# Attention and Fourier mixing on one Trainium2 core: the mixing's even column sums ahead of its odd ones, and cosine products ahead of sine products

## The chip, the cores and the metric

The kernel runs on one core of one Trainium2 chip. The metric is the time of the device for one execution, in microseconds (us). TensorE (PE in the profile, PEld for its weight loads), VectorE (DVE), ScalarE (ACT), GpSimd (POOL) and the DMA queue of SyncE (SP) work beside each other; each runs its own list of instructions in order and waits on semaphores for the others.

## What is computed

Eight batches of eight heads with 576 tokens: attention in which, per row, only scores within tau of the row's maximum are kept. The 512 columns that result per token go through a two-dimensional Fourier transform of which the real part is added, a normalization, and two matrices with a ReLU between them.

```python
scores = scale * np.matmul(q, k.transpose(0, 1, 3, 2))
thresh = np.max(scores, axis=-1, keepdims=True) - tau
scores = np.where(scores >= thresh, scores, -1000000000.0)
attn = np.exp(scores - np.max(scores, axis=-1, keepdims=True))
attn = attn / (np.sum(attn, axis=-1, keepdims=True) + 1e-09)
x = np.matmul(attn, v)                 # then (B,H,S,D) -> (B,S,H*D)
u = x + np.real(np.fft.fft(np.fft.fft(x, axis=1), axis=2))
un = (u - mean(u)) / np.sqrt(var(u) + 1e-06)
out = u + np.maximum(un @ w_ch1, 0.0) @ w_ch2
```

All data is fp32.

## The kernel before

**Order by hand.** The order on every engine is the order in which the program calls its functions; no scheduler moves anything. Generators are advanced at chosen places, so that stages of different batches interleave.

**Attention.** A pair of heads has five steps, t=0 to 4, and a batch has four pairs, so 20 steps (`per_batch`). A step i does, in the loop of the later batches: `scores(i)` (L440; L446 for t=4, which holds the leftover rows of both heads and so is half as large); `softmax_first`, the negated row maxima on VectorE (L520) and behind them the exponentials on ScalarE (L526, with the threshold at L530); `fill(True)`, a share of the matrix work of an earlier batch; `softmax_second`, the masking on VectorE (L540) and the inverse of the sum (L385, L388); the transposes of the weights of step i-1 on TensorE (L587, L605) and their copies on ScalarE (L593, L607), in two parts with a `fill()` between; `softmax_third`, the scaling (L549); at t=3 `prep_pair`, which transposes q and k of the next pair on VectorE (L408 to L411); and a last `fill`. The values are L636, their copy L643 or L645. The scores of step i+1 need the PSUM banks that the masking of step i has read.

**Mixing.** A batch's transform over 576 tokens uses symmetries. `fold_rows` adds and subtracts mirrored halves of the rows of a pair (`half`, L687) and folds them again into `f` (L692 to L703), which has four chunks p and, in each, even columns (the first FW = 304) and odd columns (the next 304). The last pair of a batch is folded on VectorE, the others on GpSimd. `mixing(b)` is a generator for the rest:

- `fold_chunks` adds and subtracts chunks 0 and 2 on VectorE (L718, L719), all 608 columns at once. Chunks 1 and 3 were done on GpSimd before.
- Five additions and folds on VectorE, of 304 columns each, put the sums into place (L744, L740 three times, L749).
- Six products `py` on TensorE (L759): three groups of rows u, for each an even one with the cosine table (three matmuls) and an odd one with the sine table (two). ScalarE copies each from PSUM (L764; for an even one also a single column, L769).
- Products over the sequence (`pa`, L776 and L780), additions on VectorE (L796, L797), and the sum with x into `u_t` (L801, L805).

Each `yield` in it is a place where other work comes between. In the later batches `start_batch` puts the mixing of the batch before into the list at t=2 of the first pair; `mix(1)` advances it by one piece behind the masking, a `fill()` by one more. The three pieces of sums go to t=2 behind the masking, to the next `fill()`, and to t=3 ahead of the masking. The first `py` follows at t=3 behind the masking.

```python
        if i % per_batch == 3:
            mix(1)
```

stands for that between `softmax_first` and `fill(True)`. For batch 0 (`second_batch`, `first == 0`) sums and products are called by hand behind the eight matmuls of `column_means` (L360); for the last batch (the tail) three `mix(1)` go between shares of the matrix work, and the rest follows when `ended` is set.

**Matrices.** Both channel products run on TensorE as two-level products with seven multiplications for eight (`ph`, L1203; `po`, L1390). Their sums are spread over the other engines: differences of halves of the hidden rows on GpSimd (L1161), sums and differences of their quarters on VectorE and GpSimd (L1184), gathering on GpSimd (L1255, L1336), partial results out of PSUM on ScalarE (L1402) or VectorE (L1410), and rows with their factor (L883, L888).

**PSUM.** `py`, `pe`, `pw`, `pv`, `pa`, `po`, `ph` share four banks (tag mm); a new tile takes a bank whose last reader has to be done. Scores have four banks of their own.

## Time and profile before

| | |
|---|---|
| median of 3 runs | 1574.97 us (1571.53 to 1575.13) |
| the profiled execution | 1571.58 us, of which the span of instructions is 1569.8 |
| mean granted TensorE clock | 0.996 |
| busy: PE, PEld | 1526.0 us, 1187.1 us |
| busy: DVE, ACT, POOL | 1061.6, 916.4, 777.5 us |
| L759 `py`: matmuls | 240, of 275 ns (median) |
| L718, L719 on DVE, 608 columns | 8 each, 0.78 and 0.79 us (median) |
| L744, L749, 304 columns | 8 each, 0.47 us (median) |
| L740, 304 columns | 24, 0.53 us (median) |

The span runs from the first to the last instruction. A line of the timeline gives the start, the duration, the engine with the line of the code, the operation, the tile written and the tiles read with their sizes, the count, and in brackets the idle time of the engine just ahead of it with what ended it. A line with a count merges equal neighbours: its duration is that of them all. A duration of VectorE can contain time in which it stood.

### The profile page before, as it was taken

Reading aid. Unit: us, or ns where it says so; the run is one execution under the profiler, and the core shown is the slowest. Engines: PE = TensorE matmul, PEld = TensorE weight load, DVE = VectorE, ACT = ScalarE, POOL = GpSimd, SP = SyncE. Lnnn points to the kernel's source line nnn. Section 1 sums busy time; section 2 is a strip of 40 time slices with the busy share of each in tenths; the row PEclk is TensorE's granted clock in tenths of the full one; section 3 lists DMA queues with packets and bytes.
Section 4 is the critical chain, followed back from the end, with each engine's and each line's share of the span. In section 5 each row is a group of like instructions: output and inputs, shape, how many; then the busy total and the mean of one; then the engine's idle time right before and its main releaser. Section 6 shows DMA issues by size and latency. Waiting matters only on the chain.

```text
span 1569.8 us, 27001 instructions
## 1 busy us (share of the span) xinstructions
PE 1526.0 (97%) x9786; PEld 1187.1 (76%) x9786; DVE 1061.6 (68%) x2119; ACT 916.4 (58%) x1921; POOL 777.5 (50%) x962
## 2 busy tenths in 40 slices
PE   8988989999999999999999999999999999999999
PEld 4555545556788778877787778877787878889999
DVE  7987776846869566776577566866577666745546
ACT  6875666554666666656766566657666666232231
POOL 3774553034455652546254724555264625546735
PEclk9999999999999999999999999999999999999999
DMA  6423231646956264634454345635464434646655
GB/s 166 130 58 117 77 90 24 204 147 180 323 154 214 73 188 122 185 111 144 144 173 149 116 135 153 184 103 158 130 185 137 141 118 149 222 141 235 235 201 182
DMA packets 248907, 239.31 MB, mean 152 GB/s; under 512 B 197027, under 2 KB 218533, under 8 KB 228678
## 3 DMA queue, kind: packets, MB, share of 16 engines
q1 hardware_dynamic: 246262, 237.28, 49.6%
q8 instruction: 78, 1.28, 0.3%
q10 hardware_dynamic: 2512, 0.30, 0.1%
q14 instruction: 55, 0.45, 0.1%
HBM read 205.93 MB, written 31.46 MB: 151 GB/s over the span
## 4 chain that ended last, share of the span: by engine, by line
PE 83%; DVE 9%; ACT 4%; issue 1%; DMA 1%; POOL 1%; SPq 0%; ACTq 0%; DVEq 0%
PE ph L1203 24%; PE po L1390 18%; PE pv L636 9%; PE sc L440 9%; PE pw L605 7%; PE po L926 4%; PE ph L902 3%; PE sc L446 2%; PE py L759 2%; PE pa L776 1%; PE pe L587 1%; DVE neg L461 1%; PE pn L851 1%; PE pa L780 1%; PE pd L111 1%
## 5 line engine op out<-in xcount | busy, mean ns | idle before, releaser
L520 DVE TENSOR_REDUCE neg<-sc 128x1 f32<-128x576 f32 x216 | 154.3, 751 | 131.4 <-PE sc L440 118.6
L526 ACT ACTIVATE e<-sc,neg 128x576 f32<-128x576 f32 x216 | 158.5, 734 | 120.7 <-DVE neg L520 120.7
L1390 PE MATMUL po<-w,w_all 128*128 128x128 f32 x1728 | 219.0, 277 | 0.3 <-ACT ends L593 0.3
L1140 DVE TENSOR_TENSOR hs<-ph,hs 128x512 f32<-128x512 f32 (+1 forms) x128 | 105.4, 823 | 161.1 <-PE ph L1203 104.0
L1390 PEld LDWEIGHTS po<-w,w_all 128*128 128x128 f32 x1728 | 204.9, 192 | 9.2 <-issue 6.2
L1149 POOL TENSOR_TENSOR w<-hs 128x512 f32<-128x512 f32 x32 | 42.1, 1320 | 317.8 <-ACT hs L1145 243.9
L540 DVE SCALAR_TENSOR_TENSOR e<-sc,thr,e 128x576 f32<-128x576 f32 x216 | 168.4, 813 | 19.9 <-ACT thr L530 19.6
L1203 PE MATMUL ph<-u_t,w 128*128 128x256 f32 x768 | 180.5, 382 | 0.6 <-DMA w<-f 0.4
L607 ACT COPY e_t<-pw 128x512 f32<-128x512 f32 x256 | 148.7, 595 | 45.8 <-PE pw L605 44.7
L605 PE MATMUL pw<-ident,e 128*128 128x128 f32 x1152 | 169.9, 275 | 5.6 <-ACT ends L593 2.2
L440 PE MATMUL sc<-kT,qT 64*128 64x288 f32 x1024 | 168.1, 431 | 6.6 <-DVE e L477 4.4
L549 ACT ACTIVATE e<-e,den 128x576 f32<-128x576 f32 x216 | 157.5, 775 | 8.5 <-DVE den L388 7.7
L1203 PEld LDWEIGHTS ph<-u_t,w 128*128 128x128 f32 x768 | 141.4, 190 | 23.2 <-issue 4.4
L1203 PE MATMUL ph<-w_all,w 128*128 128x256 f32 x672 | 157.1, 383 | 1.1 <-DVE w_all L1125 1.0
L605 PEld LDWEIGHTS pw<-ident,e 128*128 128x128 f32 x1152 | 135.4, 141 | 21.9 <-issue 5.6
L1203 PEld LDWEIGHTS ph<-w_all,w 128*128 128x128 f32 x672 | 123.6, 190 | 23.7 <-issue 4.9
L1145 ACT ACTIVATE hs<-hs 128x512 f32<-128x512 f32 (+1 forms) x96 | 74.1, 771 | 113.5 <-DVE hs L1140 112.8
L440 PEld LDWEIGHTS sc<-kT,qT 64*128 64x128 f32 x1024 | 95.7, 187 | 57.9 <-issue 26.8
L1255 POOL TENSOR_TENSOR w_all<-w_all 128x128 f32<-128x128 f32 (+2 forms) x160 | 116.9, 747 | 30.3 <-DVE w_all L1410 22.4
L1390 PE MATMUL po<-w,hs 128*128 128x128 f32 x912 | 119.4, 278 | 0.3 <-ACT ends L593 0.3
L1390 PEld LDWEIGHTS po<-w,hs 128*128 128x128 f32 x912 | 109.7, 192 | 9.7 <-issue 7.1
L801 POOL TENSOR_TENSOR u_t<-x,tmp 128x289 f32<-128x289 f32 (+1 forms) x45 | 33.9, 753 | 123.7 <-DVE tmp L796 123.7
(224 smaller groups left out, 2946.7 us busy)
## 6 DMA issues: line engine op xcount, KB each, us to landing
w<-f SPq DMA_DIRECT2D x150, 1024.0 KB, 4.9
hs<-in_moe_w_ch_dram SPq DMA_DIRECT2D x23, 512.0 KB, 5.2
q_in<-in_q_dram SPq DMA_DIRECT2D x128, 72.0 KB, 4.1
out_dram<-u SPq DMA_DIRECT2D x36, 256.0 KB, 2.3
k_in<-in_k_dram SPq DMA_DIRECT2D x124, 72.0 KB, 2.6
v_in<-in_v_dram SPq DMA_DIRECT2D x64, 128.0 KB, 5.0
f<-w SPq DMA_DIRECT2D x14, 512.0 KB, 3.9
f<-w SPq DMA_DIRECT2D x7, 1024.0 KB, 4.8
```

The costliest lines, as they stand in the source:

```text
L440: nc.tensor.matmul(sc[j][:, c, 0:HALF], qT[hp, 128 * t : 128 * t + 128], kT[hp, k0 + HALF * c : k0 + HALF * (c + 1)], start=True, stop=True,)
L520: nc.vector.tensor_reduce(out=neg[:, j : j + 1], in_=sc[j][:, :, 0:HALF], axis=AXIS_XY, op=ALU.max, negate=True,)
L526: nc.scalar.activation(out=ej, in_=sc[j][:, :, 0:HALF], func=ACT.Exp, bias=neg[:, j : j + 1], scale=1.0)
L540: nc.vector.scalar_tensor_tensor(out=ej, in0=sc[j][:, :, 0:HALF], scalar=thr[:, j : j + 1], in1=ej, op0=ALU.is_ge, op1=ALU.mult, accum_out ...
L549: nc.scalar.activation(out=e[:, S * j : S * (j + 1)], in_=e[:, S * j : S * (j + 1)], func=ACT.Copy, scale=den[:, j : j + 1],)
L605: nc.tensor.transpose(pw[:, c, :], e[:, c0 : c0 + 128], ident[:, :])
L607: nc.scalar.copy(e_t[:, 4 * j : 4 * j + 4, qs], pw[:, :, :])
L636: nc.tensor.matmul(pv[64 * j : 64 * j + 64, 0:m], vt[:, 2 * c + j, :], e_t[:, 4 * j + c, 0:m] if c < 4 else ends[:, 0, 0:m], start=(c == 0 ...
L1140: nc.vector.tensor_tensor(out=to, in0=bank, in1=to if other is None else other, op=ALU.add)
L1203: nc.tensor.matmul(bank[:, 256 * q : 256 * q + 256].rearrange("p (two n) -> p two n", two=2), left[:, 256 * c + 128 * q : 256 * c + 128 * ...
L1255: return lambda: eng.tensor_tensor(out=to, in0=to, in1=other, op=ALU.add)
L1390: nc.tensor.matmul(to, lefts[m][j][:, s], right_[:, 128 * s : 128 * (s + 1)], start=jn in (0, 4) and s == 0, stop=s == 3, skip_group_check ...
```

## The change

- `fold_chunks` gets the columns as an argument. `mixing` first sums the even columns only (two instructions of 304 columns), then does the three even folds in one piece, with the third of them moved up; the sums and folds of the odd columns (two and two instructions) stand in the third piece, and there is no `yield` between them and the first product.
- The six products come in the order cosine u=0, 1, 2, then sine u=0, 1, 2.
- The `mix(1)` at t=3 ahead of the masking goes. The third piece, with the first product, is therefore advanced by the `mix(1)` behind the masking, where the first product was.
- For batch 0 the fold of the last pair is split: the even half, the mixing's even sums, then the odd half.
- For the last batch two instead of three `mix(1)` stand between the shares of matrix work.

All else in `fold_rows` is a regrouping that issues the same instructions in the same order. The number of instructions grows by two on VectorE for each batch.

```diff
@@ fold_rows
+        if last and not late:
+            once(0)
+            twice(0)
+            middle()
+            yield
+            once(1)
+            twice(1)
+            return
@@
-    def fold_chunks(eng, b, c):
-        eng.tensor_tensor(out=sums[b][:, c, :], in0=f[:, c, :], in1=f[:, c + 2, :], op=ALU.add)
-        eng.tensor_tensor(
-            out=f[:, c + 2, :], in0=f[:, c, :], in1=f[:, c + 2, :], op=ALU.subtract
-        )
+    def fold_chunks(eng, b, c, cols=slice(0, 2 * FW)):
+        low, high = f[:, c, cols], f[:, c + 2, cols]
+        eng.tensor_tensor(out=sums[b][:, c, cols], in0=low, in1=high, op=ALU.add)
+        eng.tensor_tensor(out=high, in0=low, in1=high, op=ALU.subtract)
@@ mixing
-        fold_chunks(nc.vector, b, 0)
+        fold_chunks(nc.vector, b, 0, E)
         yield 0
...
         fold(f[:, 1, E], s01[:, 1, E], flip, s01[:, 0, E])
+        fold(f[:, 2, E], f[:, 3, E], minus, f[:, 2, E])
         yield 0
-        fold(f[:, 2, E], f[:, 3, E], minus, f[:, 2, E])
+        fold_chunks(nc.vector, b, 0, O)
         fold(f[:, 3, O], f[:, 2, O], plus, f[:, 3, O])
         nc.vector.tensor_tensor(out=f[:, 0, O], in0=s01[:, 0, O], in1=s01[:, 1, O], op=ALU.subtract)
-        yield 0
+        sums.pop(b)
...
-        for u, r, n in ((0, 0, 128), (1, 128, 48), (2, 176, 128)):
-            for odd in range(2):
+        for odd in range(2):
+            for u, r, n in ((0, 0, 128), (1, 128, 48), (2, 176, 128)):
@@ second_batch, first == 0
-            folds.append(fold_rows(n - 1))
-            while folds:
-                fold_more()
+            outer = fold_rows(n - 1)
+            next(outer)
+            start_batch(0)
+            mix(2)
+            next(outer, None)
             load_v(n + 1)
-            start_batch(0)
-            mix(3)
             mix(3)
@@ the loop of the later batches, behind softmax_first
-        if i % per_batch == 3:
-            mix(1)
@@ the tail
-        if n < 3:
+        if n < 2:
             mix(1)
```

More of the change, by code (lines that the diff above doesn't have):

```diff
@@ L685, in fold_rows, with once, twice, middle @@
         eng = nc.vector if last else nc.gpsimd
-        for c, op in enumerate((ALU.add, ALU.subtract)):
-            eng.tensor_tensor(out=half[:, c, 1:HALF], in0=up, in1=down, op=op)
-        yield
-        for c, c0, op in (
-            (0, 0, ALU.add), (0, 161, ALU.subtract), (1, FW, ALU.subtract), (1, FW + 161, ALU.add)
-        ):
-            eng.tensor_tensor(
-                out=f[:, p, c0 : c0 + mid - 1], in0=half[:, c, 1:mid],
-                in1=_reversed(half[:, c, mid + 1 : HALF]), op=op,
-            )
-            if late and last and c0 > 0 and c0 != FW:
-                yield
-        eng.tensor_tensor(
-            out=f[:, p, mid - 1 : mid + 1], in0=_stepped(x, mid, -mid, 2),
-            in1=_stepped(x, 3 * mid, -mid, 2), op=ALU.add,
-        )
-        eng.tensor_tensor(
-            out=_stepped(f[:, p, :], 160, FW, 2), in0=_stepped(x, 0, mid, 2),
-            in1=_stepped(x, HALF, mid, 2), op=ALU.subtract,
-        )
+        def once(c):
+            eng.tensor_tensor(
+                out=half[:, c, 1:HALF], in0=up, in1=down, op=(ALU.add, ALU.subtract)[c]
+            )
+        def twice(c):
+            for c0, op in zip((FW * c, FW * c + 161), (ALU.add, ALU.subtract)[:: 1 - 2 * c]):
+                eng.tensor_tensor(
+                    out=f[:, p, c0 : c0 + mid - 1], in0=half[:, c, 1:mid],
+                    in1=_reversed(half[:, c, mid + 1 : HALF]), op=op,
+                )
+        def middle():
+            eng.tensor_tensor(
+                out=f[:, p, mid - 1 : mid + 1], in0=_stepped(x, mid, -mid, 2),
+                in1=_stepped(x, 3 * mid, -mid, 2), op=ALU.add,
+            )
+            eng.tensor_tensor(
+                out=_stepped(f[:, p, :], 160, FW, 2), in0=_stepped(x, 0, mid, 2),
+                in1=_stepped(x, HALF, mid, 2), op=ALU.subtract,
+            )
+        if last and not late:
[6 more added lines that the diff above has]
+            return
+        once(0)
+        once(1)
+        yield
+        twice(0)
+        if late and last:
+            yield
+        twice(1)
+        if late and last:
+            yield
+        middle()
         yield
@@ L715, in fold_halves @@
         fold_chunks(nc.gpsimd, b, 1)
-    def fold_chunks(eng, b, c):
-        eng.tensor_tensor(out=sums[b][:, c, :], in0=f[:, c, :], in1=f[:, c + 2, :], op=ALU.add)
-        eng.tensor_tensor(
-            out=f[:, c + 2, :], in0=f[:, c, :], in1=f[:, c + 2, :], op=ALU.subtract
-        )
+    def fold_chunks(eng, b, c, cols=slice(0, 2 * FW)):
+        low, high = f[:, c, cols], f[:, c + 2, cols]
+        eng.tensor_tensor(out=sums[b][:, c, cols], in0=low, in1=high, op=ALU.add)
+        eng.tensor_tensor(out=high, in0=low, in1=high, op=ALU.subtract)
     MIX = 4 * (3 * 5 * 128 + 5 * 2 * KH)
@@ L734, in mixing @@
         E, O = slice(0, FW), slice(FW, 2 * FW)
-        fold_chunks(nc.vector, b, 0)
+        fold_chunks(nc.vector, b, 0, E)
         yield 0
-        s01 = sums.pop(b)
+        s01 = sums[b]
         def fold(out_, in0, factor, in1):
```

## The prediction

> **What bounds the kernel.** I read the engines' busy times first, then TensorE's waits, then the timeline around one mixing.

> ```profile
> PE 1526.0 (97%) x9786; PEld 1187.1 (76%) x9786; DVE 1061.6 (68%) x2119; ACT 916.4 (58%) x1921; POOL 777.5 (50%) x962
> ```

> TensorE sets the time and the change takes none of its matmuls away, so it can only win TensorE's idle time. In the answer on TensorE's waits (us in total, times, longest) two rows concern the mixing:

> ```profile
> PE py L759 <- DVE f L740: 8.8, 5, 2.0
> ...
> PE py L759 <- DVE w_all L1410: 1.6, 1, 1.6
> ```

> The eight mixings begin at 132, 309, 505, 675, 848, 1020, 1191 and 1363 us. Asked for by window, the five waits on f are those of 505 (1.2), 675 (1.5), 848, 1020 and 1191 (2.0 each). 675 adds 0.7 for a PSUM bank (L605 behind L1410) and 1363, the tail, has the 1.6. **Ceiling: 8.8 + 0.7 + 1.6 = 11.1 us**, 0.7%. The timeline of the mixing at 1191, where t=2, 3, 4 are steps of the loop (start, us, engine, line):

> ```profile
> 1190.98 1.42 DVE L520 TENSOR_REDUCE neg<-sc 128x1 f32<-128x576 f32 x2
> 1191.09 0.56 PE L759 MATMUL py<-dim_c,f 128*128 128x65 f32 x4
> 1191.21 2.08 POOL L1336 TENSOR_TENSOR w_all<-w_all 128x896 f32<-128x896 f32 x1 [4.37 <-DVE w_all L1410]
> ...
> 1192.31 1.75 DVE L740 SCALAR_TENSOR_TENSOR f<-f,factors 128x304 f32<-128x304 f32 x2
> ...
> 1193.67 0.49 PE L759 MATMUL py<-dim_c,f 128*128 128x128 f32 x2 [2.03 <-DVE f L740]
> ...
> 1193.99 0.46 DVE L749 TENSOR_TENSOR f<-sums 128x304 f32<-128x304 f32 x1
> ...
> 1197.42 0.77 DVE L408 STREAM_TRANSPOSE kT<-k_in 128x576 f32<-128x576 f32 x1
> ...
> 1197.86 1.28 POOL L1184 TENSOR_TENSOR w_all<-hs 128x512 f32<-128x512 f32 x1 [4.57 <-PE po L1390]
> ...
> 1199.18 0.72 DVE L520 TENSOR_REDUCE neg<-sc 128x1 f32<-128x576 f32 x1
> 1200.00 0.74 ACT L526 ACTIVATE e<-sc,neg 128x576 f32<-128x576 f32 x1 [1.08 <-DVE neg L520]
> ...
> 1201.07 0.63 ACT L764 COPY y_o<-py 48x256 f32<-48x256 f32 x1
> ```

> TensorE stands at the third matmul of the first cosine product until VectorE has folded the last even columns. But VectorE shows no idle from 1184 to 1200.5: it is late by itself. Its maximum of t=4 (1199.18) releases ScalarE's exponential (1200.00), behind which the sine copy (1201.07) stands; the next product then waits 0.26 us for that copy's bank, at 1201.75. **TensorE's pace is set a second time there, by VectorE.**

> [...]

> ```profile
> 498.06 1.46 POOL L1184 TENSOR_TENSOR w_all<-hs,w_all 128x512 f32<-128x512 f32 x1
> 498.31 1.87 DVE L718 TENSOR_TENSOR sums<-f 128x608 f32<-128x608 f32 x1
> 499.49 1.82 POOL L1161 TENSOR_TENSOR hs<-hs,w 128x512 f32<-128x512 f32 x1
> 500.21 1.75 DVE L719 TENSOR_TENSOR f<-f 128x608 f32<-128x608 f32 x1
> ```

> L718 takes 0.78 elsewhere, L1161 1.27: each stood until the other had ended, and the waiting one goes before the next of its rival. Maskings (L540, 804 to 822 ns over 216) and transposes (L408, 767 to 778) never stretch: the first read one input from PSUM, the second have one. [...] from start to start it is 0.39 us (L744) against 0.81 (L718): split is not dearer.

> **The change, part by part, at 1191.** Start to start: 0.40 for an addition of 304 columns, 0.45 for a fold with a factor.

> 1. *t=2.* Two sums of 608 (1.63) become two of 304 (0.80); the fold of f2 joins (0.45). VectorE saves 0.4. Since it is late, the maximum of t=3, its exponentials and the copies behind them come 0.4 earlier.
> 2. *t=3 ahead of the masking.* Two folds and one addition go: 1.3 us. The part of L740 that is blocking (1.75 for two of 0.53: 0.8) does not go: L1184, next in line with two SBUF inputs, meets the same L1336. The masking comes some 1.6 earlier, at 1193.3.
> 3. *t=3 behind the masking.* Two additions, a fold, an addition: +1.7. Queued behind them are the transposes for the next pair (not needed by TensorE before t=0, 1205) and the maximum of t=4. **Sum of 1 to 3: -0.4 - 1.3 + 1.7 = 0.0.** The maximum of t=4 stays at 1199.2.
> 4. *Product order.* The first cosine product no longer waits (2.0). The second takes the bank of the first (so the built kernel's order and waits have it), whose copies stand behind the exponential of t=3: that ends at about 1193.0, two copies 0.7, so it starts at 1193.7, where the first sine product started at 1194.9. Three cosine products then hold 0.3 more of matmuls than cosine, sine, cosine. Scores of t=4: 1196.5 against 1197.55, **1.0 won**.
> 5. *t=4.* The first sine product needs the odd sums (done 1197.5; it comes at 1199.4): no wait. The second needs the bank of the first, whose copy stands behind the exponential of t=4: no earlier than 0.15 before now. With the 0.3 of matmuls already done, **of 2.0 won at the wait 0.45 is left**.
> 6. *The lock.* L1184 on POOL waits for the po matmuls ahead of the scores. With TensorE 1.0 earlier it asks at 1196.85. The odd sums run from 1195.8 to 1197.5, the last starting at 1197.07; now, only transposes run there. If it gets in, the last sum waits for it (some 1.1), and with it transposes, maximum, exponential, sine copy: the second sine product starts 1.0 late, less 0.3 already done: **0.7 lost**. The margin is 0.2 us, less than I can compute; both ends stand.

> The other places: 505, 848 and 1020 run alike (848 had a half clock in this profile; I count it like the others). At 675 the second sine product waits for L1410, behind the same maximum: 0.0, within 0.2. At 309 VectorE waits for TensorE: -0.1.

> At 132 the last fold_rows of batch 0 is split too. Even side from 128.4: 0.4 + 0.5 + 0.25 for the first half, 0.8 + 1.3 for the sums, so 131.7; TensorE comes at 132.65, after eight matmuls of L360. Odd side 0.4 + 0.5 + 1.7 more, 134.3; it is wanted at 134.8. That saves a wait of 0.4, but the weights' transposes behind (138.41) wait for a sine copy behind the exponentials of the next step, as now: -0.15.

> Tail: the 1.6 goes, as the folds (1358.9 to 1362.2) leave the place ahead of L1410: the bank is free near 1360, TensorE comes at 1361.35. 0.65 for the product, 1.9 for 16 matmuls of L1390, 1.35 for two cosine products: the first sine product is wanted at 1365.3. But the odd sums, from 1361.1, now take turns with L1184 and L1255 on POOL (the latter 2.07 each): they end at 1361.95, 1364.3, 1366.7 and 1367.5. Three sine products (0.45 each) and their copies later, the first pa that reads the last copy starts at 1369.8, now 1369.15: +0.65, from -1.0 (the lock spares the sums) to +1.9 (one more turn).

> SP's and POOL's order is unchanged; no DMA is moved past another.

> Sum: four places at -0.45 to +0.66, that is -1.8 to +2.6; the rest -0.15 - 0.1 + 0.0 + 0.65 = +0.4. **-1.4 to +3.0, middle +0.8**. I take +1: the profiled execution (span 1569.8, 1571.58 with what lies around it) would take 1572.6; the median shown is 3.4 above it, so **1576**.

> **Rivals.**
> *A, the waits are simply saved.* For it: six waits with named causes, all removed. Against: the copy at 1201.07. It holds if the sine banks come free without the exponential of t=4, or VectorE gains 0.7 at each place that I do not see. About three quarters of 11.1: -8, 1567.
> *B, the odd sums collide.* Place: behind the masking of t=3, against L1184; in the tail against L1255. Each of five places then gives VectorE's full 1.1 on to TensorE (5.5), the tail 2.7: +8, 1583. It decides from the point where L1184 asks before the last odd sum has begun. For it: L718 to L719 above, and step 6. Against: 0.3 of matmuls done earlier and TensorE's 0.15 cushion take some back.
> *C, it does not do what it says.* The built order shows the products and sums moved as described, so at most a few per cent.

> **How the numbers follow.** About 0.3% (4.7 us) is what a measurement of this kernel can tell from no change. Handed back, 0.62: all of -1.4 to +3.0 lies within. A 0.15, faster. B 0.20, slower. C 0.03, within. Rounded: faster 0.15, same 0.64, slower 0.21. The range 1567 to 1583 reaches to the centres of A and B and leaves out half of each, under 0.2; the likeliest case alone spans 1573.5 to 1578.

> **What would show it.** Right: the row py from L740 gone from TensorE's waits; the maximum of t=4 0.4 us further from that of t=3, or 1.5 where L1184 gets in; TensorE's or its weight load's wait for a sine copy or L1410 in t=4, 1 us or more. Odd sums stretched to 1.5 us mark step 6. Wrong: the exponential of t=4 released 1 us or more earlier (A), or new waits of py on f of over 1 us outside the tail (B).

## The result, and the profile after

| | before | changed |
|---|---|---|
| median | 1574.07 us of 6 runs (1571.53 to 1575.13) | 1579.96 us of 6 runs (1578.2 to 1581.71) |
| profiled execution, span | 1571.58, 1569.8 us | 1580.4, 1578.6 us |
| mean granted TensorE clock | 0.996 | 0.991 |

The ratio is 1.0038, with a 95% interval of 1.0025 to 1.0051: **slower by 0.38%**. That lies in the range given, but above the likeliest case's own (1573.5 to 1578), on rival B's side: it is a loss that can be told from no change, and the likeliest forecast was none. In this section "after" is the changed kernel; most of its lines are those of before plus 20 (`py` L779, `pw` L605 as before, `po` L1410, L1430 for L1410, POOL's and VectorE's L1204 for L1184, the sums L739 and L740, the folds L759, L763, L769).

The busy times of the page of after, and three rows of TensorE's waits (us in total, times, longest), to be held against the two groups shown of before:

```profile
PE 1530.5 (97%) x9786; PEld 1191.3 (75%) x9786; DVE 1067.9 (68%) x2135; ACT 917.3 (58%) x1921; POOL 777.6 (49%) x962
```

```profile
PE pw L605 <- DVE w_all L1430: 9.2, 5, 2.0
PE py L779 <- ACT y_e L789: 4.9, 6, 1.3
...
PE py L779 <- DVE f L769: 1.5, 2, 1.1
```

The span grew by 8.8 us. TensorE has the same 9786 matmuls, but is busy 4.5 us longer, and stands 4.3 us longer (1578.6 - 1530.5 = 48.1 against 1569.8 - 1526.0 = 43.8). These are two different losses. The row `py` from L740 (8.8 us) is gone, as the change intends. In its place stand two others: the second cosine product waits for the copy `y_e` that frees its bank, and a `pw` waits for L1430, 2.0 us in t=4 at four places (505, 850, 1023, 1197). The fifth wait of that row, 1.12 us at 678.95, is already in t=3, behind the first cosine product.

**Where the idle time comes from.** The mixing at 1197, which is the one at 1191 of before (timeline of after: start, duration, engine with line; the bracket is the idle time ahead with what ended it):

```profile
1196.62 1.41 DVE L520 TENSOR_REDUCE neg<-sc 128x1 f32<-128x576 f32 x2
...
1196.91 0.83 PE L779 MATMUL py<-dim_c,f 128*128 128x65 f32 x6
...
1199.59 0.65 PE L779 MATMUL py<-dim_c,f 128*48 128x65 f32 x6 [1.29 <-ACT y_e L789]
...
1201.85 0.47 DVE L739 TENSOR_TENSOR sums<-f 128x304 f32<-128x304 f32 x1
1202.22 1.14 PE L446 MATMUL sc<-kT,q_ends 128*128 128x288 f32 x4
1202.35 0.47 DVE L740 TENSOR_TENSOR f<-f 128x304 f32<-128x304 f32 x1
1202.53 1.43 POOL L1204 TENSOR_TENSOR w_all<-hs 128x512 f32<-128x512 f32 x1 [3.60 <-PE po L1410]
...
1202.86 1.43 DVE L759 SCALAR_TENSOR_TENSOR f<-f,factors 128x304 f32<-128x304 f32 x1
...
1204.22 0.46 DVE L769 TENSOR_TENSOR f<-sums 128x304 f32<-128x304 f32 x1
1204.60 0.76 DVE L408 STREAM_TRANSPOSE kT<-k_in 128x576 f32<-128x576 f32 x1
...
1206.35 0.72 DVE L520 TENSOR_REDUCE neg<-sc 128x1 f32<-128x576 f32 x1
1206.99 0.67 DVE L1430 TENSOR_TENSOR w_all<-w_all,po 128x512 f32<-128x512 f32 x1
...
1207.72 0.66 PE L605 MATMUL pw<-ident,e 128*128 128x128 f32 x4 [2.02 <-DVE w_all L1430]
```

Read it from below. TensorE stands at 1207.72 for a bank that L1430 reads out. L1430 is behind the maximum of t=4, that behind the transposes, those behind the odd sums. POOL's L1204 came at 1202.53 into the middle of the odd sums, and the fold L759 stood until POOL had done (POOL at 1203.96, the fold at 1204.29): 1.43 us where it takes 0.53 alone (0.54 at 675, where POOL did not come). The maximum of t=4 begins 9.73 us behind that of t=3; before it was 8.20 (1190.98 to 1199.18).

What the place costs as a whole shows between two points with the same matmuls between them: the scores of the step ahead of the mixing's first product, and the scores five steps later (us of the stretch, then busy us and number of instructions of PE, PEld, DVE, ACT, POOL, then the granted clock, the DMA share and GB/s; first before, then after):

```profile
1185.60:1231.89 46.29, 43.92 (x324) 35.67 (x324) 29.64 (x67) 26.88 (x57) 23.16 (x29) 1.00 0.35 104
1191.42:1240.29 48.87, 45.15 (x325) 37.06 (x324) 30.92 (x69) 26.79 (x57) 23.36 (x29) 0.97 0.33 99
```

TensorE is idle for 2.37 us before and 3.72 after, 1.35 more. The other three places of this kind give 1.27 to 1.36, together 5.3; the remaining four mixings take back 1.0 (0.7 of it at 675), which makes the 4.3.

**Where the busy time comes from.** The timeline's stretch at 1197 cut into the windows in which the clock is granted (columns as above):

```profile
1202.86:1206.27 3.41, 2.84 (x24) 2.49 (x22) 3.37 (x5) 0.47 (x2) 2.09 (x2) 1.00 0.00 0
1206.27:1209.68 3.41, 1.69 (x12) 1.26 (x13) 2.54 (x7) 2.37 (x6) 0.27 (x1) 1.00 0.50 83
1209.68:1213.10 3.42, 3.42 (x18) 3.42 (x17) 0.00 (x0) 2.27 (x5) 0.00 (x0) 0.50 0.59 97
1213.10:1216.51 3.41, 3.41 (x28) 2.81 (x27) 1.98 (x3) 0.78 (x2) 2.04 (x1) 1.00 0.00 0
```

In the window with the wait TensorE is busy 1.69 us of 3.41. In the next one it runs at half the clock: always busy, but with 18 matmuls instead of 28. In this trace such a window follows a wait for L1430 at all five middle mixings of after (those at 505, 677, 850, 1023 and 1197); in that of before only one follows a middle mixing, that of 848.

What one such window costs shows where nothing else differs: e4 below has the middle mixings of before unchanged, and a half-clock window at 675 where before has none (first before, then e4):

```profile
669.38:716.07 46.69, 44.48 (x332) 36.36 (x331) 30.05 (x63) 25.75 (x56) 25.34 (x29) 1.00 0.37 107
669.71:717.92 48.21, 46.00 (x332) 37.70 (x331) 30.05 (x63) 26.36 (x56) 25.32 (x29) 0.96 0.35 103
```

The idle time is 2.21 us in both, the stretch 1.52 longer: **1.5 us for a window**. Four more of them are 6 of the 8.8 us between the two profiled executions; the other 2.8 are the changed waits and order.

The number of windows changes from one execution of a kernel to the next. e1, e4 and e5 keep the waits for L740 at the middle mixings as before, and their traces have two, two and three half-clock windows behind these. The granted clock of before was 0.996 in the profiled execution, but 0.9948 on average in the 27 runs beside e1 to e4; that of after was 0.991, but 0.9928 on average in its six runs. A window at half clock is 0.0011 of the span (3.41 / 2 / 1573), so between average runs the difference is about two windows, an estimate: some 3 of the 5.9 us by which the medians differ.

### The profile page after: what moved, and what is told of

Same layout as the page of the kernel before. It is cut to its first block, busy times and chain, and to the rows that moved or that the text cites. A ratio compares the mean times of both kernels' runs of the same rounds, so it can differ in the third digit from the quotient of the medians.

```text
span 1578.6 us, 27022 instructions
## 1 busy us (share of the span) xinstructions
PE 1530.5 (97%) x9786; PEld 1191.3 (75%) x9786; DVE 1067.9 (68%) x2135; ACT 917.3 (58%) x1921; POOL 777.6 (49%) x962
## 3 DMA queue, kind: packets, MB, share of 16 engines
q8 instruction: 78, 1.28, 0.3%
## 4 chain that ended last, share of the span: by engine, by line
PE 81%; DVE 10%; ACT 4%; DMA 2%; issue 1%; POOL 1%; SPq 0%; DVEq 0%; ACTq 0%; POOLq 0%
PE ph L1223 24%; PE po L1410 18%; PE pv L636 9%; PE sc L440 9%; PE pw L605 6%; PE po L946 4%; PE ph L922 2%; PE sc L446 2%; DVE neg L461 1%; PE pa L796 1%; DVE neg L520 1%; PE pn L871 1%; DVE e L540 1%; PE pe L587 1%; PE pa L800 1%
## 5 line engine op out<-in xcount | busy, mean ns | idle before, releaser
L520 DVE TENSOR_REDUCE neg<-sc 128x1 f32<-128x576 f32 x216 | 154.1, 750 | 130.4 <-PE sc L440 118.8
L526 ACT ACTIVATE e<-sc,neg 128x576 f32<-128x576 f32 x216 | 158.7, 735 | 135.6 <-DVE neg L520 135.6
L1410 PE MATMUL po<-w,w_all 128*128 128x128 f32 x1728 | 221.8, 279 | 0.6 <-DMA w<-f 0.3
L1410 PEld LDWEIGHTS po<-w,w_all 128*128 128x128 f32 x1728 | 208.4, 195 | 9.0 <-issue 5.6
L605 PE MATMUL pw<-ident,e 128*128 128x128 f32 x1152 | 171.5, 276 | 13.6 <-DVE w_all L1430 9.2
L540 DVE SCALAR_TENSOR_TENSOR e<-sc,thr,e 128x576 f32<-128x576 f32 x216 | 168.3, 812 | 19.9 <-ACT thr L530 19.8
L605 PEld LDWEIGHTS pw<-ident,e 128*128 128x128 f32 x1152 | 134.9, 141 | 33.3 <-DVE w_all L1430 10.4
L1275 POOL TENSOR_TENSOR w_all<-w_all 128x128 f32<-128x128 f32 (+2 forms) x160 | 117.4, 751 | 42.8 <-DVE w_all L1430 34.9
L1410 PE MATMUL po<-w,hs 128*128 128x128 f32 x912 | 119.9, 279 | 0.0
L1410 PEld LDWEIGHTS po<-w,hs 128*128 128x128 f32 x912 | 110.4, 193 | 9.2 <-issue 7.0
```

The costliest lines, as they stand in the source:

```text
L520: nc.vector.tensor_reduce(out=neg[:, j : j + 1], in_=sc[j][:, :, 0:HALF], axis=AXIS_XY, op=ALU.max, negate=True,)
L526: nc.scalar.activation(out=ej, in_=sc[j][:, :, 0:HALF], func=ACT.Exp, bias=neg[:, j : j + 1], scale=1.0)
L540: nc.vector.scalar_tensor_tensor(out=ej, in0=sc[j][:, :, 0:HALF], scalar=thr[:, j : j + 1], in1=ej, op0=ALU.is_ge, op1=ALU.mult, accum_out ...
L605: nc.tensor.transpose(pw[:, c, :], e[:, c0 : c0 + 128], ident[:, :])
L1275: return lambda: eng.tensor_tensor(out=to, in0=to, in1=other, op=ALU.add)
L1410: nc.tensor.matmul(to, lefts[m][j][:, s], right_[:, 128 * s : 128 * (s + 1)], start=jn in (0, 4) and s == 0, stop=s == 3, skip_group_check ...
```

## The experiments

Theory V, formed from these lines: the loss is made at the five middle places, on VectorE's way to the maximum of t=4 (odd sums, POOL in their midst, transposes), and the half-clock windows are a consequence of the waits there. Rivals: the order of the products with its waits for `y_e` (P), the tail (T), the clock as chance (K). Ratios are to the kernel before, of the runs beside it, with 95% intervals; 0.3% is about what can be told from no change.

| kernel | median us | ratio to before |
|---|---|---|
| e1 order of products alone | 1573.4 | 1.0007 [0.9994, 1.0021] |
| e2 changed, odd sums left out | 1563.18 | 0.9938 [0.9925, 0.9950] |
| e3 changed, transposes behind t=4 | 1566.08 | 0.9959 [0.9947, 0.9971] |
| e4 change in first and last batch alone | 1573.35 | 0.9998 [0.9987, 1.0009] |
| e5 before, transposes behind t=4 | 1572.64 | 0.9991 [0.9979, 1.0004] |
| e6 changed, wait filled (first way) | 1591.06 | 1.0108 [1.0085, 1.0130] |
| e7 changed, odd sums behind transposes | 1573.85 | 0.9996 [0.9984, 1.0008] |
| e8 changed, products in the old order | 1601.6 | 1.0178 [1.0154, 1.0202] |
| e9 changed, wait filled (second way) | 1576.0 | 1.0018 [1.0009, 1.0026] |
| e10 e3, first product ahead of exponentials | 1565.49 | 0.9952 [0.9938, 0.9966] |

### Which part: order, sums, ends

**e1**, the order of the products alone, on the kernel before:

```diff
-        for u, r, n in ((0, 0, 128), (1, 128, 48), (2, 176, 128)):
-            for odd in range(2):
+        for odd in range(2):
+            for u, r, n in ((0, 0, 128), (1, 128, 48), (2, 176, 128)):
```

> The kernel before with the order of the products changed alone (cosine u=0, 1, 2, then sine); the sums stay at their three places. Theory V (VectorE's way to the maximum of t=4 is what costs, and the lock with POOL on the odd sums): nothing stands behind the masking of t=3, the maximum of t=4 stays 8.2 us behind that of t=3, TensorE still waits for L740 some 8 to 9 us in all, and no new wait for L1410 appears: 1573 to 1577 us. Rival P (the order of the products is the cost, since the second and third cosine products wait for banks that ScalarE frees late): the waits for y_e and the half-clock stretches of the changed kernel appear here as well: 1578 to 1581 us.

No difference, and the row of waits for L740 as in the kernel before, to the digit:

```profile
PE py L759 <- DVE f L740: 8.8, 5, 2.0
```

The waits for `y_e` are 0.9 us in all, five of at most 0.2, against 0.7 before. The 1.3 us of the changed kernel is therefore not a cost that the order adds: the second cosine product starts when ScalarE has freed its bank, and the first product's old wait hid that. Rival P falls.

**e8**, the other half alone: the changed kernel with the two loops as in the kernel before (the diff of e1 the other way round).

> The changed kernel with the products in the old order (cosine and sine by turns); the sums are split and moved as in the change. Theory V: the second product is now a sine one, which TensorE reaches behind the transposes of t=2's weights while the odd sums are done only 4 to 5 us later; the wait of py for f (the row of the last odd addition) is 3 to 5 us at each of five places, partly instead of the waits for L1430 that follow: 1583 to 1600 us. Rival: the order of the products does not matter with the sums moved: 1578 to 1581 us.

```profile
PE py L779 <- DVE f L769: 32.4, 8, 5.6
```

The second product is then a sine one and stands up to 5.6 us for the odd sums. The time is 1.6 us beyond the upper end. So the moved sums need the new order, which alone costs nothing that can be measured (e1).

**e4**, the change in the first and last batch alone:

```diff
-        fold_chunks(nc.vector, b, 0, E)
+        split = b in (0, B - 1)
+        fold_chunks(nc.vector, b, 0, E if split else slice(0, 2 * FW))
...
+        if i % per_batch == 3:
+            mix(1)
```

> The change is made for the first and the last batch alone (sums, products and the split fold of batch 0; the tail with two pieces); the six batches between are as in the kernel before. Theory V: the places in the loop make the cost, so this is the kernel before less 0.2 at batch 0 and plus 0.6 to 1.6 in the tail: 1574 to 1576 us. Rival T (the tail makes it, odd sums against POOL's L1275): 1578 to 1580 us.

1573.35 is 0.7 below V's lower end, and the ratio is 0.9998: the ends cost nothing that can be measured. Rival T falls; the loss lies in the mixings between.

### What delays the maximum of t=4

**e2**, without the two odd sums:

```diff
-        fold_chunks(nc.vector, b, 0, O)
         fold(f[:, 3, O], f[:, 2, O], plus, f[:, 3, O])
-        nc.vector.tensor_tensor(out=f[:, 0, O], in0=s01[:, 0, O], in1=s01[:, 1, O], op=ALU.subtract)
+        nc.vector.tensor_tensor(out=f[:, 0, O], in0=f[:, 0, O], in1=s01[:, 1, O], op=ALU.subtract)
```

> The changed kernel without the two sums of odd columns (L739, L740 of the third piece); the odd folds then take what is in f, so the odd half of the transform is not the reference's. Theory V: VectorE is 0.8 us less behind the masking of t=3 and POOL's addition can no longer stand in the middle of four instructions, so the maximum of t=4 comes 0.8 us (POOL still gets in) to 1.9 us (it does not) earlier; the 9.2 us of waits of pw for L1430 fall to 1 to 5, and with them the additional half-clock stretches: 1568 to 1574 us. Rival P (order of the products): 1578 to 1580 us, the 4.9 us of waits for y_e unchanged. Rival T (tail): the five places do not change the time by more than 2 us.

**e3**, the transposes of q and k of the next pair behind the masking of t=4; nothing is left out:

```diff
-            if t == 3 and n + 1 < B * NPAIR:
+            if t == 3 and n + 1 < B * NPAIR and i % per_batch != 3:
                 prep_pair(n + 1)
...
             softmax_second(i)
+        if i % per_batch == 4:
+            prep_pair(n + 1)
```

> The changed kernel with the three transposes of q and k (L408 to L411) of the first pair of each batch moved from t=3, ahead of the maximum of t=4, to behind the masking of t=4; nothing is left out. Theory V: 1.8 us go from VectorE's way to the maximum of t=4, so the 9.2 us of waits for L1430 fall under 2 us and the additional half-clock stretches behind them go: 1566 to 1572 us, below the kernel before, unless the scores of the next t=0 then wait for the transposes (in that case TensorE shows a wait for L408 or L411, up to 1 us at each of six places, and the time is 1570 to 1576). Rival P: the waits for y_e stay and the time with them, 1578 to 1580. Rival K (the clock's half-speed stretches are chance, not bound to waits): they appear in the same number as in the changed kernel, and no more than the idle time is won, 1570 to 1572.

Two different things are taken from the same path, and both times the wait in t=4 goes. The distance from the maximum of t=3 to that of t=4 at the last middle mixing, and the row of `pw` for L1430 (its line differs by kernel):

| kernel | distance | waits of pw, us in all |
|---|---|---|
| after | 9.73 | 9.2 |
| e7 | 8.90 | 2.6 |
| e3 | 7.97 | 2.3 |
| e2 | 7.81 | 1.1 |

In every row 1.1 us are the wait in t=3 of the mixing at 677, which none of these edits touches. What is left for each of the other four places is 2.0, 0.4, 0.3 and 0.

The timeline of e3, at the place that stood for 2.02 us:

```profile
1191.15 1.43 DVE L759 SCALAR_TENSOR_TENSOR f<-f,factors 128x304 f32<-128x304 f32 x1
...
1192.50 0.46 DVE L769 TENSOR_TENSOR f<-sums 128x304 f32<-128x304 f32 x1
1192.88 0.75 DVE L520 TENSOR_REDUCE neg<-sc 128x1 f32<-128x576 f32 x1
...
1193.55 0.67 DVE L1430 TENSOR_TENSOR w_all<-w_all,po 128x512 f32<-128x512 f32 x1
...
1194.28 0.66 PE L605 MATMUL pw<-ident,e 128*128 128x128 f32 x4 [0.29 <-DVE w_all L1430]
```

POOL still stretches the fold to 1.43, but with the transposes away the maximum follows the last addition at once. And the waits for `y_e` are the same 4.9 us as in after, while the time is 0.8% lower: once more against P. e2 went further than expected (1568 was the lower end): its TensorE busy time is 8.2 us below that of after (1522.3 against 1530.5), and no half-clock window is left behind a middle mixing. I had put that into the expectation with too small a size.

e3 is **faster than the kernel before by 0.41%** and than the changed one by 0.8% (0.9959 to 1.0038). Its page shows both losses undone, 7.7 us less busy (1522.8) and 6.4 less idle (1564.5 - 1522.8 = 41.7) than after (one half-clock window is left at a middle mixing, that at 672, where the wait in t=3 stays):

```profile
PE 1522.8 (97%) x9786; PEld 1185.8 (76%) x9786; DVE 1069.9 (68%) x2135; ACT 917.4 (59%) x1921; POOL 777.4 (50%) x962
```

**e5**, the same move of the transposes on the kernel before (the diff of e3):

> The kernel before with the three transposes of q and k of the first pair of each batch moved behind the masking of t=4, and nothing else. Theory V: before the change the maximum of t=4 sets TensorE's pace only by the 0.3 us that a sine product waits for a copy, and the 8.8 us of waits for L740 stand earlier, so 0 to 2 us are won: 1571 to 1574 us. Rival M (the move of the transposes is what won in the changed kernel, whatever the order of sums and products): 1564 to 1567 us.

Nothing measurable; the 8.8 us for L740 stand as they were. Rival M falls. So neither edit wins alone: the change takes away the wait at t=3, the move takes away the one that follows at t=4, and only both together bring time.

**e7**, the odd sums behind the transposes, still ahead of the maximum of t=4:

```diff
+        swap = 0 < b < B - 1
+        if not swap:
+            odd_side()
...
+                if swap and not odd and u == 2:
+                    odd_side()
                 py = ps.tile([128, 512], FP32, tag="mm", bufs=4, name="py")
```

`odd_side` holds the four instructions on the odd columns; its definition is left out here.

> The changed kernel with the odd sums and folds of the six middle batches behind the transposes of q and k at t=3 instead of ahead of them; the maximum of t=4 stays behind both, nothing is left out. POOL's L1204 then asks while VectorE transposes. Theory V with the lock: the odd fold is no longer stretched (0.5 us instead of 1.4 for two), the maximum of t=4 comes 8.6 us behind that of t=3 instead of 9.7, the waits for L1430 fall from 2.0 to about 1 us a place, and the first sine product waits up to 0.5 us for the sums: 1571 to 1577 us. Rival (the lock costs nothing, the four instructions alone make the delay): distance 9.7 or more, 1579 to 1582 us.

The timeline of e7 at the same place:

```profile
1197.12 0.77 DVE L408 STREAM_TRANSPOSE kT<-k_in 128x576 f32<-128x576 f32 x1
...
1197.81 1.28 POOL L1213 TENSOR_TENSOR w_all<-hs 128x512 f32<-128x512 f32 x1 [3.60 <-PE po L1419]
...
1199.96 0.54 DVE L759 SCALAR_TENSOR_TENSOR f<-f,factors 128x304 f32<-128x304 f32 x1
...
1200.80 0.75 DVE L520 TENSOR_REDUCE neg<-sc 128x1 f32<-128x576 f32 x1
```

VectorE does the same instructions in another order. POOL's addition meets transposes, takes its 1.28, and the fold takes 0.54. The distance is 8.90 instead of 9.73 (8.6 was expected), and the first sine product waits 0.61 us for the sums: **the lock is worth 0.83 us of the path here**, and taking it away brings the kernel back to the time of before. TensorE's idle time falls by less than the waits for L1430, by 1.9 us (46.2 against 48.1), since the waits of `py` for the sums grow from 1.5 to 5.7 us; its busy time falls by 3.9, with one half-clock window at a middle mixing instead of five. This kernel is what the prediction called handed back.

### What the clock is worth

**e6** was to fill the wait of 2.0 us with transposes of the identity, into a part of the tile `pe` that nothing reads:

```diff
+        if i >= 60 and i % per_batch == 3:
+            for c in range(7 if i // per_batch == 4 else 14):
+                nc.tensor.transpose(pe[:, 2 + c % 2, :], ident[:, :], ident[:, :])
```

> The changed kernel with 63 transposes of the identity more on TensorE, into a part of a PSUM tile that nothing reads, at t=4 of the five mixings that wait: 14 each ahead of the pw that waits 2.0 us for L1430 (some 0.13 us each, 1.8 us), 7 at the one that waits 1.1. They fill the wait and lengthen it by nothing, or by up to 0.2 us a place. Theory C (the half-clock stretches of 3.41 us follow a stretch in which TensorE stood for over about half of it): the five additional stretches are gone, and with each some 0.9 to 1.7 us: 1572 to 1576 us. Rival K (chance, or bound to something else): the stretches stay and the time is 1580 to 1581 us.

It failed as an instrument. The copy of `pe` to `ends` stands ahead of these writes in the program, and in the trace they wait for it:

```profile
PE pe L600 <- ACT ends L593: 15.1, 5, 3.1
```

Up to 3.1 us idle instead of 2.0, and the fill behind it: slower by 1.1%. It decides nothing between C and K, but three of its five waits, of some 3 us, were followed by no half-clock window; the wait was split between two windows there. At 1214, for one, the windows had 1.74 and 2.04 us of busy time.

**e9** put the fill into the tile of the first sine product, ahead of its copy:

```diff
+                if odd and u == 0 and 1 < b < B - 1:
+                    for _ in range(7 if b == 3 else 14):
+                        nc.tensor.transpose(py[:, 256:384], ident[:, :], ident[:, :])
                 y = y_o if odd else y_e
```

> The fill once more, now into columns of the first sine product's own PSUM tile that nothing reads, ahead of that tile's copy: 63 transposes of the identity, 14 (some 1.8 us) ahead of the pw that waits 2.0 us for L1430 at four places, 7 where it waits 1.1. The copy of that tile stands behind the exponential of t=4 and ends no earlier than the fill, so nothing should wait for the fill: the wait for L1430 falls from 2.0 to about 0.2. Theory C (a half-clock stretch follows a stretch of 3.41 us in which TensorE was busy for little over half): the five additional stretches are gone, each worth 0.9 to 1.7 us: 1572 to 1576 us. Rival K: the stretches stay, 1580 to 1582 us.

The wait is 0.5 us at each of the four places that waited 2.0, and none of the five windows is left. At the fifth place the fill stands in t=4, behind the wait of t=3, which stays at 1.13 us: that this window is gone too is not the work of the fill. TensorE is busy for 1533.9 us, of which the 63 transposes are some 8.1 (63 x 0.128, from 1.15 us for nine): 1525.8 without them, 4.7 below after. The windows of e9 over that stretch:

```profile
1202.81:1206.23 3.42, 3.19 (x29) 2.95 (x28) 3.38 (x7) 0.28 (x1) 1.29 (x1) 1.00 0.02 5
1206.23:1209.64 3.41, 2.86 (x23) 2.44 (x24) 1.36 (x5) 3.27 (x8) 0.00 (x0) 1.00 0.72 118
1209.64:1213.05 3.41, 3.41 (x29) 2.81 (x28) 1.51 (x3) 1.25 (x4) 1.42 (x1) 1.00 0.35 58
```

A kernel with more work on TensorE is faster by 0.2%, some 3 us: 1.0018 against 1.0038, with intervals that overlap by a hair. The median is at the upper end of what C gave. The granted clock says the same over all runs, 0.9963 on average in the 15 of e9 and 0.9928 in the six of after. In the traces the span is 1.9 us shorter (1576.7 to 1578.6): 4.7 less busy without the fill, 2.8 more of idle time and fill together (1576.7 - 1525.8 = 50.9 against 48.1). Theory C holds for the four places with the fill. That the fill is no cure is plain beside e3, which has nothing to fill.

### One step further

**e10** is e3 with the first cosine product ahead of the exponentials of t=3, so that its copy finds ScalarE idle:

```diff
+        if i % per_batch == 3:
+            mix(1)
         if i < total:
             softmax_first(i)
...
-        if mixes:
+        if mixes and i % per_batch != 3:
             mix(1)
```

The odd sums stand where they stand in e3, by the function of e7.

> The changed kernel with the transposes of q and k behind the masking of t=4 as above, and besides the first cosine product of each middle mixing at t=3 ahead of the exponentials of t=3 instead of behind the masking, so that its copy goes ahead of those exponentials on ScalarE, which stands idle there. Nothing is left out. Theory B (the 4.9 us that the second cosine product waits for the bank come from the copy queued behind the exponentials): the waits for y_e fall under 1.5 us and 2 to 4 us more are won: 1562 to 1565 us. Rival: the copy delays the exponentials or the matrix work that is now split another way waits instead: 1566 to 1570 us.

The row of waits for `y_e` is gone, so its cause was the one named; the win that was expected with it is not shown, the time is 0.5 us above B's range and e3's within the intervals. TensorE's idle time is 39.2 us against 41.7, but it is busy 2.7 longer. At the last middle mixing, between the same scores, it is idle 0.9 less and busy 0.7 more (45.32 us with 44.20 busy, e3 45.46 with 43.48). Why its matmuls take longer stays open.

## Why the prediction was right or wrong

- **The bound**: right. TensorE lost or won what stood in the way of its matmuls, and its second wait in t=4, behind VectorE's maximum, was the one that decided. e3 against e5 shows both waits one after the other.
- **Steps 1 to 3** (VectorE's balance): right where L1184 gets in, too small by 0.3 without it. The maximum of t=4 was to be 0.4 us further from that of t=3, or 1.5: 8.20 became 9.73, and 8.90 without the lock (e7). One reading in them is wrong: 0.40 from start to start was taken from L744 for all additions of 304 columns. The split sums take 0.50 (1201.85, 1202.35 and 1202.86 above), so two of 304 cost 1.0 where one of 608 cost 0.81. Split is dearer by some 0.2, near the difference of the durations before (medians: twice 474 ns for 304 columns, 780 for 608, so 168 ns), where the prediction took split as not dearer.
- **Step 4** (second cosine product at the bank; scores of t=4 1.0 earlier): right. The scores come 5.31 us behind the first product (1202.22 - 1196.91), before 6.46 (1197.55 - 1191.09). The wait for the bank is the 1.29 us at 1199.59.
- **Step 5**: the 0.45 left per place is not shown. e7, which has no lock there, loses a little instead: at the last middle mixing, between the same scores, it takes 46.41 us where before takes 46.29. But it has a wait of its own for the sums, so it is not the change without the lock.
- **Step 6** (the lock): the mechanism with its place was right, the choice was not. The margin of 0.2 us was less than the working could resolve, and I took the middle of both ends. POOL got in at all four places named alike (505, 850, 1023, 1197: L759 takes 1.43 each), and not at 675 (0.54), where 0.0 was forecast. The price was too small: at 850, where both traces have a half-clock window, the stretch between the same scores is 0.88 us longer (48.52 against 47.64), and at the three others 2.5 to 2.6, of which the window is 1.5. So about 1.0 a place, where the loss end had 0.66. What stands longest is not the sine product but a `pw` behind L1430, the other of the two waits named in the tests.
- **The term that was missing** is the clock. The sum counted what TensorE waits and saves at full clock; half-clock windows behind the waits are no step of it. With both ends of step 6 at loss it gave +3.0. The profiled executions differ by 8.8, of which four windows are about 6 and the rest 2.8, close to that end; of the 5.9 between the medians about 3 are the clock. So the +1 failed at two steps: the lock was put at the middle of its two ends, where the loss end came, and the clock was put at nothing. That the sum of the rest comes so close is in part luck: about 1.0 a place instead of 0.66 is made up by the other four mixings, which win some 1.3 in all where +0.4 was forecast.
- **The tail**: +0.65 was forecast, between -1.0 and +1.9. From the last scores to the end of the span it takes 246.7 us (1578.6 - 1331.91), before 246.3 (1569.8 - 1323.51): +0.4, near the forecast. The 1.6 of waiting ahead of its first product is gone; in its place two of the four instructions on the odd columns are stretched by POOL (1.84 and 2.24 us), and `py` waits 1.1 us for L769. e4 has the same +0.4 in its trace, and no loss that its runs can tell.
- **Batch 0**: -0.15 was forecast, at the weights' transposes of 138.41. They start at 137.93, 0.5 earlier, but not for the reason given: the wait for the odd columns, which was to go, is still 0.45.
- **Rival A** falls by the new rows. **Rival B**, with 0.20, is what came in place and sign; its 1583 was too high by 3. At 675 the lock did not come and the tail did not take 2.7, but the clock, which B does not have either, makes about half of the loss. The new waits of `py` on `f` outside the tail that were to mark B are not there.
- **The range** held because it reached to the centre of rival B. The case taken as likeliest, no measurable difference at 0.62, did not come.

## What to carry to other kernels

A wait that is taken away shows the next one, and that one decides what is won: follow the freed engine to its next wait before you count. Here the cure was to take work that nobody awaits (the transposes) off the path to that next wait, and it was worth nothing that can be measured without the change and 0.8% with it. If an addition of another engine asks amid a row of instructions with two SBUF inputs and the margin is a few tenths of a us, do not take the middle: put one-input instructions there, as e7 did (0.4%; beside POOL's addition the transpose kept its 0.77 us, where the fold took 1.43 for 0.53).

## What the runs showed of the hardware

| TensorE busy in the window | windows | next one at half clock |
|---|---|---|
| under 1.3 us | 23 | 23 |
| 1.3 to 1.7 | 21 | 15 |
| 1.7 to 2.1 | 54 | 14 |
| over 2.1 | 5084 | 2 |

No wait of the changed kernel's middle mixings is longer than 2.03 us, and a half-clock window followed at all five. At 859 to 861 one wait of 2.03 us lay whole in a window; at 678 waits of 1.12 and 0.38 us in one window were enough. A wait of 2.0 us can so cost 1.5 us more than it lasts (1.52 in e4). How the grid cuts the waits differs from trace to trace: the kernel before has waits of 2.03 and 1.51 us at t=3, with 1.92 us of work in the window at 1192 and 1.94 at 673, and no half-clock window followed there, while e5, with the same waits for L740 (8.8 us in all), has 1.75 and 1.38 us of work in its windows there, and one at half clock behind each. The table has no sharp limit: between 1.3 and 2.1 us of work both outcomes occur.
